# Two fused transformer layers on one core: one weight matrix loaded in four pieces, constant matmuls at three places, another order of the row loads

## The chip, the core and the metric

The kernel runs on one core of a Trainium2 chip. The engines have names of their own in the profile: PE is TensorE (matrix products, with PEld for its weight loads), DVE is VectorE, ACT is ScalarE, POOL is GpSimd, SP is SyncE, which here only issues transfers. DMA transfers are issued from the queues of SP, POOL and ACT. The metric is the device time of one execution in microseconds (us); the median of three runs is compared.

## The reference, cut to what matters

```python
def A(x, mem0, Wq, Wk, Wv, Wo):            # x [2048,512], mem [8,512], 32 heads of 128
    mem = mem0
    for s in range(64):                     # segments of 32 tokens
        h = concat([mem, x[32*s : 32*s+32]])                    # 40 rows
        q, k, v = h @ Wq, h @ Wk, h @ Wv                        # per head
        p = softmax(where(mask, q @ k.T * 128**-0.5, -1e9))     # token rows causal, memory rows over all
        o = (p @ v) @ Wo
        mem = o[:8];  out[s] = o[8:]
def B(x, wqkv, wo):                         # 32 heads of 16, no causal mask
    q, k, v = split(x @ wqkv)
    phi = lambda t: where(t > 0, t + 1, exp(t)) + 1e-6
    kv, z = sum_s phi(k) v^T, sum_s phi(k)
    return (phi(q) @ kv / (phi(q) . z + 1e-6)) @ wo
x = x + A(layernorm(x));  x = x + B(layernorm(x))               # layer 0
x = x + A(layernorm(x));  x = x + B(layernorm(x))               # layer 1, same weights
```

The mask is `(row < 8) | (row >= column)`. The eight memory rows go from segment to segment, so the 64 segments of A are a serial chain in each layer. B needs all rows of x before it can give any.

## The kernel before, in words

**Work and names.** Each layer has 64 steps, one per segment. A step projects rows of its segment to keys and queries (`kq0`, `kq1`: two halves of 16 heads), projects values (`v`), does the attention of the memory rows (`mem0`, `mem1`, the function `mem_attention`), gives the output rows by Wo (`out`) and writes the new memory rows (`next`, the function `next_mem`). This is the chain. Beside it run the attention of the token rows (`x`, the function `x_attention`), which nothing in the chain waits for, the residual (`res`), and the "left" blocks (`left0`, `left1`, `leftv`): keys, queries and values of the last 8 tokens of four segments, 32 rows made at once for a tile of 128 rows; a step's own projections take the 8 memory rows and the other 24. B is spread over the steps: after every fourth step a finished tile of 128 rows goes through `b_in` (layernorm, keys, values and queries by wqkv, running sums kva and za). After the last tile `b_mid` folds kva into wo and forms zf from za; `b_out` then gives the rows tile by tile. In layer 0 these outputs are spread over the steps of layer 1; in layer 1 all sixteen tiles come at the end (lines 2785 to 2821). For some tiles ("late") the queries are not done in `b_in`: the normalized rows are stored (`xn_scratch`) and read back transposed.

**Tiles.** A projection of 32 rows runs as groups of four matmuls, each on 32 columns of the array and 512 wide (lines 2154 and 2042; 2042 is the same with weights already in the array). Results are in one of eight PSUM banks and are copied by ScalarE (line 1919) or VectorE (line 1920). VectorE transposes 32x32 blocks (line 2173). Weights of A, 4 MB each, stay in SBUF; Wo comes in sixteen pieces of 256 KB, wqkv in one load of 1.5 MB.

**What sets the order.** The table `PLACE` (lines 16 to 1547) has for every operation a number, and a letter `a` or `v` where ScalarE or VectorE was chosen for a copy. The operations are emitted on each engine in the order of these numbers (`schedule`, line 1673); the numbers are no waits, and an engine runs its instructions in order. The bank of a tile is the least recently used one in that order. Semaphore waits follow from reads and writes. The numbers `lat` and `lands` in the code were used when the table was made, and have no effect on the program that is emitted.

**Opening.** SP issues Wk, Wq, Wv, the pieces of Wo and wqkv in this order (`load`, line 1951). ScalarE issues mem0, then x tile 0 (lines 1946, 1947); GpSimd issues x tile 1 after four constants and x tile 2 three constants later (line 1936). Then come the layernorms of these tiles, their transposes on TensorE (line 2109), and the key and query projections of the left blocks of tiles 0 to 2 (`first_left_blocks`: `sk` and `sq`) mixed with those of segment 0.

**End.** `last_rows` issues on SP, once Wq and Wk are no longer needed, transposed loads into their places: the stored queries of tiles 0 to 3 (`pq`, line 2754), the stored rows of the late tiles 4 to 7 (`xn`, line 2746), `pq` of tiles 8 to 11 and of 12 to 14, then the rows of x in four loads (`xs`, line 2753). `last_queries` makes the queries of tiles 4 to 7. The same queue carries the `dx` loads, which move rows of the output `y_sb` to the place where the residual (line 2485) adds them. The last tile's `b_in` needs the last memory step, `b_mid` needs the last tile, and the products of line 2718 and the rows of `b_out` follow.

## Time and profile before

| what | value |
|---|---|
| median of 3 runs | 1581.24 us (1580.29 to 1581.54) |
| the profiled execution's own time | 1580.13 us |
| its span | 1578.4 us |
| mean granted clock of TensorE | 0.997 |
| TensorE busy | 1511.5 us, 96% |
| VectorE busy | 1223.1 us, 77% |
| ScalarE busy | 987.4 us, 63% |
| landing of Wk, Wq, Wv after issue | 13.7, 24.4, 34.1 us |
| wqkv, issue to landing | 10.0 us |
| first key projection | 16.27 us |
| first product of line 2718 in the end | 1552.30 us |

The span is the time between the first and the last instruction in the profile; 1.7 us of the execution lie outside it. Busy time is the sum over instructions of an engine. The granted clock is 1.00 when TensorE runs at full speed. Rows of windows give, for a stretch of time, the busy time of each engine with its number of instructions in brackets, the granted clock, the DMA share and the rate.

### The profile page before, as it was taken

Reading aid. Unit: us, or ns where it says so; the run is one execution under the profiler, and the core shown is the slowest. Engines: PE = TensorE matmul, PEld = TensorE weight load, DVE = VectorE, ACT = ScalarE, POOL = GpSimd, SP = SyncE. Lnnn points to the kernel's source line nnn. Section 1 sums busy time; section 2 is a strip of 40 time slices with the busy share of each in tenths; the row PEclk is TensorE's granted clock in tenths of the full one; section 3 lists DMA queues with packets and bytes.
Section 4 is the critical chain, followed back from the end, with each engine's and each line's share of the span. In section 5 each row is a group of like instructions: output and inputs, shape, how many; then the busy total and the mean of one; then the engine's idle time right before and its main releaser. Section 6 shows DMA issues by size and latency. Waiting matters only on the chain.

```text
span 1578.4 us, 97381 instructions
## 1 busy us (share of the span) xinstructions
PE 1511.5 (96%) x48481; PEld 822.8 (52%) x40705; DVE 1223.1 (77%) x3536; ACT 987.4 (63%) x3043; POOL 197.2 (12%) x396
## 2 busy tenths in 40 slices
PE   5899999999999999999999999999999999999997
PEld 2445555555555555555545555555555455555554
DVE  4577878887777788777878787888877787777778
ACT  2566665656666666665666666666576666576665
POOL 2011110111111011111111110111101011110110
PEclk9999999999999999999999999999999999999999
DMA  9301010110000000101310111111101111001124
GB/s 381 104 20 20 17 33 20 27 24 23 21 18 16 22 24 24 24 17 30 62 32 17 26 25 20 25 29 21 31 10 27 27 27 23 23 20 20 34 42 134
DMA packets 84819, 60.69 MB, mean 38 GB/s; under 512 B 64121, under 2 KB 78777, under 8 KB 82873
## 3 DMA queue, kind: packets, MB, share of 16 engines
q1 hardware_dynamic: 71096, 37.58, 9.7%
q0 software_dynamic: 13152, 16.75, 3.9%
q8 instruction: 349, 5.72, 1.5%
q14 instruction: 62, 0.50, 0.1%
q10 hardware_dynamic: 160, 0.14, 0.0%
HBM read 25.57 MB, written 11.67 MB: 24 GB/s over the span
## 4 chain that ended last, share of the span: by engine, by line
PE 83%; DVE 8%; ACT 4%; DMA 3%; issue 1%; POOL 0%; SPq 0%; DVEq 0%
PE pb L2154 31%; PE pb L2042 21%; PE pb L2408 18%; PE pb L2054 8%; PE pb L2582 2%; ACT arena_sb L1919 2%; DMA Wq_sb<-in_A_Wq_dram 2%; PE pb L2270 1%; DMA dx_sb<-y_sb 1%; DVE arena_sb L1920 1%; PE pb L2347 1%; PE pb L2436 1%; DVE arena_sb L2173 1%; DVE y_sb L2419 1%; DVE st_sb L2092 1%
## 5 line engine op out<-in xcount | busy, mean ns | idle before, releaser
L1919 ACT ACTIVATE arena_sb<-pb 128x512 bf16<-128x512 f32 (+5 forms) x1180 | 530.8, 483 | 320.4 <-PE pb L2042 162.1
L1920 DVE CAST arena_sb<-pb 128x512 bf16<-128x512 f32 (+4 forms) x591 | 297.7, 512 | 93.7 <-PE pb L2042 51.1
L2154 PE MATMUL pb<-Wk_sb,arena_sb 128*32 128x512 bf16 x4192 | 364.4, 383 | 5.5 <-ACT arena_sb L1919 3.3
L2408 PE MATMUL pb<-Wo_sb,arena_sb 128*32 128x256 bf16 x10368 | 337.6, 273 | 4.4 <-DVE arena_sb L2318 2.1
L2173 DVE STREAM_TRANSPOSE arena_sb<-arena_sb 128x256 f32<-128x256 f32 x640 | 266.2, 432 | 48.7 <-ACT arena_sb L1919 41.2
L2054 PE MATMUL pb<-arena_sb 128*32 128x128 bf16 (+2 forms) x10800 | 277.0, 208 | 14.8 <-DVE arena_sb L1920 4.9
L2408 PEld LDWEIGHTS pb<-Wo_sb,arena_sb 128*32 128x32 bf16 x10368 | 258.1, 96 | 48.7 <-DVE arena_sb L2318 14.7
L1936 POOL DMA_DIRECT2D dx_sb<-y_sb x246 | 125.3, 513 | 1152.4 <-DVE y_sb L2419 627.0
L2054 PEld LDWEIGHTS pb<-arena_sb 128*32 128x32 bf16 x10800 | 190.1, 95 | 147.5 <-issue 33.3
L2154 PE MATMUL pb<-Wq_sb,arena_sb 128*32 128x512 bf16 x3088 | 259.5, 382 | 1.5 <-DMA Wq_sb<-in_A_Wq_dram 0.4
L2042 PE MATMUL pb<-Wv_sb,arena_sb 128*32 128x512 bf16 x2560 | 251.6, 378 | 0.1
L2154 PE MATMUL pb<-Wv_sb,arena_sb 128*32 128x512 bf16 x2560 | 251.5, 378 | 0.1
L2154 PEld LDWEIGHTS pb<-Wk_sb,arena_sb 128*32 128x32 bf16 x4192 | 112.9, 97 | 193.2 <-issue 102.6
L2042 PE MATMUL pb<-Wq_sb,arena_sb 128*32 128x512 bf16 x2032 | 199.3, 380 | 0.0
L2154 PEld LDWEIGHTS pb<-Wq_sb,arena_sb 128*32 128x32 bf16 x3088 | 83.8, 97 | 97.2 <-issue 44.4
L1919 ACT ACTIVATE outW_sb<-pb 64x256 f32<-64x256 f32 x142 | 53.6, 378 | 106.0 <-PE pb L2408 90.1
L2419 DVE TENSOR_TENSOR y_sb<-pb,outW_sb 64x256 bf16<-64x256 f32 x162 | 68.7, 424 | 50.1 <-ACT outW_sb L1919 45.4
L2358 DVE TENSOR_TENSOR arena_sb<-arena_sb,bo_sb 128x512 bf16<-128x512 bf16 x256 | 103.5, 416 | 2.4
L2318 DVE TENSOR_TENSOR arena_sb<-pb,arena_sb 128x128 bf16<-128x128 f32 x252 | 72.9, 290 | 36.3 <-ACT arena_sb L2306 12.2
L2154 PEld LDWEIGHTS pb<-Wv_sb,arena_sb 128*32 128x32 bf16 x2560 | 70.5, 95 | 53.6 <-issue 29.5
L2042 PE MATMUL pb<-Wk_sb,arena_sb 128*32 128x512 bf16 x928 | 92.5, 379 | 0.0
L2293 DVE TENSOR_TENSOR arena_sb<-arena_sb 128x256 bf16<-128x256 bf16 x252 | 70.2, 281 | 24.2 <-ACT arena_sb L2285 21.1
(122 smaller groups left out, 1804.9 us busy)
## 6 DMA issues: line engine op xcount, KB each, us to landing
Wk_sb<-in_A_Wk_dram SPq DMA_DIRECT2D x1, 4096.0 KB, 13.7
Wq_sb<-in_A_Wq_dram SPq DMA_DIRECT2D x1, 4096.0 KB, 24.4
Wv_sb<-in_A_Wv_dram SPq DMA_DIRECT2D x1, 4096.0 KB, 34.1
Wo_sb<-in_A_Wo_dram SPq DMA_DIRECT2D x16, 256.0 KB, 7.4
xs_scratch<-x_sb POOLq DMA_DIRECT2D x32, 128.0 KB, 2.7
pq_scratch<-arena_sb POOLq DMA_DIRECT2D x27, 128.0 KB, 2.5
x_sb<-xs_scratch POOLq DMA_DIRECT2D x16, 128.0 KB, 3.3
dx_sb<-y_sb SPq DMA_DIRECT2D x126, 12.0 KB
```

The lines of the kernel that those rows point to most:

```text
L1919: return e.activation(o() if callable(o) else o, i() if callable(i) else i, ACTF.Copy)
L1920: return e.tensor_copy(o() if callable(o) else o, i() if callable(i) else i)
L1936: add(eng, lambda e: e.dma_start(o, i), 0.55 if eng == "pool" else 0.66, reads=reads, writes=writes, dsem="%s%d" % (kind, k), lat=lat + (0 ...
L2042: return pe.add_instruction(mybir.InstMatmult(name=nc.get_next_instruction_name(), engine=mybir.EngineType.PE, ins=[pe.lower_ap(x), pe.low ...
L2054: r = pe.matmul(o[q], w[:, q], x, start=start, stop=stop, skip_group_check=True, tile_position=(0, 32 * j))
L2154: r = pe.matmul(o, blk[:, c, :], w, start=(c == 0), stop=(c == 3), tile_position=(0, 32 * j))
L2173: add("dve", lambda v: v.transpose(dst, src(img[:, k, :].bitcast(F32))), 0.445, reads=[("img", k, h) for h in range(2)], writes=[dkey])
L2293: add("dve", lambda v: v.tensor_tensor(Pm[:, k, :].rearrange("p (a j x) -> p a j x", a=2, j=4), PQ[:, r2, b, 0:64].rearrange("p (a x) -> p ...
L2318: add("dve", lambda v: v.tensor_tensor(oTb[:, s % NO, 16 * b:16 * b + 16, 0:8].rearrange("p (i j) q -> p j i q", i=4), heads(pv.f32()[:, 0 ...
L2358: add("dve", lambda v, b=b: v.tensor_tensor(Pbx[:, :, b, :].rearrange("p j (k x) -> p j k x", k=4), px[:, b, :].rearrange("p (k x) -> p k ...
L2408: r = pe.matmul(tl.f32()[32 * j:32 * j + 32, 0:256], oT[:, 4 * hh + n, :], Wo_sb[:, 8 * n + hh, 256 * d:256 * d + 256], start=(hh == 0 and ...
L2419: add("dve", lambda e: e.tensor_tensor(y, tl.f32()[a, 0:256], outW[c, v, :], ALU.add), c_dve(256), reads=[("outW", w), "y0"], tiles=[tl], ...
```

## The change

1. wqkv is no longer loaded by one transfer behind Wo. Four transfers of 384 KB are issued on SP, none before `next_mem` of segment 0, 1, 2 or 3 of layer 0, and each waits for the one before. On SP the first stands behind the transposed load of step 6's `prepare`, the second and third behind the `dx` load of step 2, the fourth behind those of step 4 and ahead of the transposed load of the first `b_in`.
2. `spin` is rewritten and called. One unit is twelve matmuls of 128x512 on a constant tile of ones, whose result nobody reads. Eight units stand ahead of the first key projections and wait for x tile 0; four stand between the keys and the queries of the opening; two ahead of the products of `b_mid` in layer 1; two (`spin2`) ahead of the first row output of layer 1.
3. In `last_rows` the load of the late rows (`xn`) is issued first, ahead of all `pq`.
4. `PLACE` has new numbers in steps 0 to 22 of layer 0 and from step 41 of layer 1 on; between them the order on each engine is the same as before. Some copies move between ScalarE and VectorE there. In the opening, ScalarE issues x tile 0 ahead of mem0, and GpSimd issues x tiles 2 and 1 ahead of all constants.

TensorE has 6639 scheduled operations instead of 6623, VectorE 3529 instead of 3536, ScalarE 3052 instead of 3045, SP 370 instead of 373, GpSimd 392 as before. The diff without the table; of the table the entries of three places are shown, ahead of it.

```diff
+    (0, -3, 'spin'): '12342 12989 14375 15100 15105 15679 16327 16974',
+    (0, 0, 'ldqkv'): '66837',
-    (0, 0, 'sk'): '19390 21116 22196 23282 23707v 24430',
+    (0, 0, 'sk'): '17622 17837 18269 18919 19230v 21508',
-    (0, 0, 'sq'): '29183 29399 30910 31773 32197a 32838',
+    (0, 0, 'sq'): '27549 29276 29923 30571 32514a 32731',
...
@@ -1959,7 +1967,7 @@
         for n in range(4):
             hs = slice(8 * n + 2 * i, 8 * n + 2 * i + 2)
             load(Wo_sb[:, hs, :], A_Wo[hs].rearrange("h e d -> e h d"), ("Wo", i, n), 36.45 + 3.0 * i + 0.75 * n, "dWo%d" % i)
-    load(wqkv_sb[:, :, :], B_wqkv.rearrange("(c p) f -> p c f", p=128), "wqkv", 51.5)
+    P.count += 1
 
     def load_wo_b(n):
         add("pool", lambda e: e.dma_start(MB_sb[:, :, :], B_wo.rearrange("(c p) f -> p c f", p=128)), 1.1, after=[late[-1]],
...
@@ -2054,27 +2062,27 @@
                 r = pe.matmul(o[q], w[:, q], x, start=start, stop=stop, skip_group_check=True, tile_position=(0, 32 * j))
         return r
 
-    SPIN = {}
     LATE = {0: (8, 9, 10, 11, 12, 13, 6, 7, 4, 5), 1: (4, 5, 6, 7)}
-    def spin(layer, step, name, units, cols=512, fresh=0):
+    def spin(layer, step, name, n, after=(), reads=(), fresh=1):
 
         P.at(layer, step, name)
-        tl = P.tile()
-
-        def mm(pe):
-            x = one_sb[:, 0:128].unsqueeze(1).to_broadcast([128, cols // 128, 128])
-            for i in range(units):
-                for j in range(4):
-                    o, q = tl.f32()[32 * j:32 * j + 32, 0:cols], slice(32 * j, 32 * j + 32)
-                    if 4 * i + j < 4 + fresh:
-                        r = pe.matmul(o, one_sb[:, q], x, start=True, stop=True, skip_group_check=True, tile_position=(0, 32 * j))
-                    else:
-                        r = again(pe, o, one_sb[:, q], x, True, True, (0, 32 * j), True)
-            return r
-        before = [o for o in P.nodes[-40:] if o.engs == ("pe",)]
-        nd = add("pe", mm, units * (cols / 2.4 + 3.0) * 1e-3, reads=["one"], tiles=[tl])
-        nd.order.update(before)
-        return nd
+        for i in range(n):
+            tl = P.tile()
+
+            def mm(pe, tl=tl):
+                x = one_sb[:, 0:128].unsqueeze(1).to_broadcast([128, 4, 128])
+                for u in range(3):
+                    for j in range(4):
+                        o, q = tl.f32()[32 * j:32 * j + 32, 0:512], slice(32 * j, 32 * j + 32)
+                        if u < fresh:
+                            r = pe.matmul(o, one_sb[:, q], x, start=True, stop=True, skip_group_check=True, tile_position=(0, 32 * j))
+                        else:
+                            r = again(pe, o, one_sb[:, q], x, True, True, (0, 32 * j), True)
+                return r
+            nd = add("pe", mm, c_pe(3, 512), reads=["one"] + list(reads), tiles=[tl])
+            nd.order.update(after)
+            after = [nd]
+        return after
 
     ln_no = [0]
 
...
@@ -2210,11 +2218,21 @@
 
         def first_left_blocks():
 
+            done = []
+            last = spin(0, -3, "spin", 8, reads=[("x", 0)], fresh=3)
             for W, key, move, nm in ((Wk_sb, "Wk", left_keys, "sk"), (Wq_sb, "Wq", left_queries, "sq")):
                 for G in range(3):
                     for b in range(2):
                         at(2 * G + b, nm)
+                        n0 = len(P.nodes)
                         move(G, b, project(hTL[lroom(G)], [("hTl", lroom(G))], (W, key, b, True))[0])
+                        pe = [n for n in P.nodes[n0:] if n.engs == ("pe",)]
+                        if G == 0:
+                            for n in pe:
+                                n.order.update(last)
+                            done += pe
+                if nm == "sk":
+                    last = spin(0, -1, "spin", 4, done)
             for G in range(2):
                 at(4 * G - 2, "leftv")
                 left_values(G)
...
@@ -2548,6 +2566,11 @@
             w_of[s] = out_block(s)
             if s + 1 < NSEG:
                 next_mem(s)
+            if first and s < 4:
+                nd = P.nodes[-1]
+                at(s, "ldqkv")
+                add("sp", lambda e, s=s: e.dma_start(wqkv_sb[:, s, :], B_wqkv.rearrange("(c p) f -> p c f", p=128)[:, s, :]), 0.45,
+                    after=[nd], writes=["wqkv"], dsem="dqkv%d" % s, lat=4.0)
             if s > 0:
                 residual((s - 1) // 4, (s - 1) % 4, w_of[s])
                 if g == 0:
...
@@ -2694,6 +2717,9 @@
 
     def b_mid(layer, step):
 
+        hold = []
+        if layer == 1:
+            hold = spin(layer, step, "spin", 2, [n for n in P.nodes[-40:] if n.engs == ("pe",) and n.key[2] == "bi"])
         P.at(layer, step, "bm")
         km, kk = half(qTl[:, 0], 1), ("qTl", 0, 1)
         add("dve", lambda v: v.tensor_tensor(km.rearrange("p (c m x) -> p c m x", c=4, m=4),
...
@@ -2716,7 +2742,7 @@
         for c in range(4):
             tl = P.tile()
             add("pe", lambda pe, c=c, tl=tl: tiled(pe, tl.f32()[:, :], km[:, 128 * c:128 * c + 128], MB_sb[:, c, :], True, True),
-                c_pe(1, 512), reads=[kk, ("MB", c)], tiles=[tl])
+                c_pe(1, 512), reads=[kk, ("MB", c)], tiles=[tl]).order.update(hold)
             evac(MB_sb[:, c, :], lambda tl=tl: tl.f32()[:, :], 512, tiles=[tl], writes=[("MB", c)])
 
 
...
@@ -2738,14 +2764,14 @@
         rows = [n for n in P.nodes if n.key[:3] == (1, step - 1, "lr") and n.engs == ("dve",)]
 
         prev = None
-        for w, (vw, nm, free, t0) in enumerate(((pq_view, "pq", [], 3.4), (xs_view, "xs", rows, 3.4))):
-            for i in range(0, NT - 1, 4):
+        for w, (vw, nm, free, t0) in enumerate(((pq_view, "pq", [], 7.5), (xs_view, "xs", rows, 5.0))):
+            for i in sorted(range(0, NT - 1, 4), key=lambda i: w or i not in LATE[1]):
                 n = min(4, NT - 1 - i)
                 P.at(1, step + i // 4, "ld" + nm)
                 if not w and i in LATE[1]:
                     nd = add("sp", lambda e, i=i: e.dma_start_transpose(XN(i), xn_view[i:i + 4].rearrange("t p d -> (t p) d")), 2.6,
                              reads=[("xn", t) for t in range(i, i + 4)], writes=[("RE", i), ("RE", i + 1)], after=P.res["Wk"][1],
-                             dsem="dlxn%d" % i, lat=4.8)
+                             dsem="dlxn%d" % i, lat=8.0)
                     if prev is not None:
                         nd.order.add(prev)
                     prev = nd
...
@@ -2754,7 +2780,7 @@
                          if w else (lambda e, vw=vw, i=i, n=n: e.dma_start_transpose(
                              XQ[:, :, i:i + n, :].rearrange("p c t x -> p c (t x)"), vw[i:i + n].rearrange("t p d -> (t p) d"))), 0.6 if w else 2.6,
                     reads=[(nm, t) for t in range(i, i + n)], writes=[("XE", w, t) for t in range(i, i + n)],
-                    after=P.res["Wq"][1] + free, dsem="dl%s%d" % (nm, i), lat=t0 + 0.22 * i)
+                    after=P.res["Wq"][1] + free, dsem="dl%s%d" % (nm, i), lat=t0)
                 if prev is not None:
                     nd.order.add(prev)
                 prev = nd
...
@@ -2788,7 +2814,12 @@
                 y = tiled(pe, td.f32()[:, o], zf_sb[:, c, :], e[:, c, :], True, True)
             return y
         qk = [("XQ", t // 4 * 4, fc) for fc in range(4)] if last and t in LATE[1] else []
-        add("pe", md, c_pe(4, 128), reads=["zf"] + ek + qk, tiles=[td])
+        nd = add("pe", md, c_pe(4, 128), reads=["zf"] + ek + qk, tiles=[td])
+        hold = []
+        if last and t == 0:
+            c, place = P.count, P.place
+            hold = spin(layer, step, "spin2", 2, [nd])
+            P.place, P.count = place, c
         if not last and t == 0:
             was = [n for key in rk for n in [P.res[key][0]] + P.res[key][1] if n is not None] if all(key in P.res for key in rk) else []
             for h in range(2):
...
@@ -2814,7 +2845,7 @@
         add("dve", lambda v: v.tensor_tensor(e, e, quarters(rb), ALU.mult), c_dve(512), reads=ek + rk + qk, writes=ek)
         for c in range(4):
             add("pe", lambda pe, c=c: tiled(pe, ty.f32()[:, :], e[:, c, :], MB_sb[:, c, :], c == 0, c == 3),
-                c_pe(1, 512), reads=ek + [("MB", i) for i in range(4)], tiles=[ty])
+                c_pe(1, 512), reads=ek + [("MB", i) for i in range(4)], tiles=[ty]).order.update(hold)
         add("dve", lambda v: v.tensor_tensor(x, x, ty.f32()[:, :], ALU.add), c_dve(512), reads=[xk], writes=[xk],
             tiles=[ty])
         if last:
```

3060 rows, old and new, of the table PLACE are left out of this document.

## Prediction

> **What bounds the kernel now.** I read the page first, then the windows and the chain of waits of the first 60 us, then the same for the last 50 us, and last the seam between the re-ordered and the untouched part. The page:
>
> ```profile
> span 1578.4 us, 97381 instructions
> PE 1511.5 (96%) x48481; PEld 822.8 (52%) x40705; DVE 1223.1 (77%) x3536; ACT 987.4 (63%) x3043; POOL 197.2 (12%) x396
> ...
> q8 instruction: 349, 5.72, 1.5%
> ...
> PE 83%; DVE 8%; ACT 4%; DMA 3%; issue 1%; POOL 0%; SPq 0%; DVEq 0%
> ```
>
> TensorE is the bound: 1511.5 of 1578.4 us busy, 83% of the chain that ended last. Removing work of other engines buys nothing in the middle; what can be won is TensorE's 67 us of idle time and its slow clock, and most of both lies at the two ends. Instructions come in packets of 5.72 MB / 349 = 16 KB. The windows of the opening (TensorE, weight loads, VectorE, ScalarE, GpSimd, then granted clock, DMA share, GB/s):
>
> ```profile
> 24.00:26.00 2.00, 0.85 (x13) 0.24 (x17) 0.93 (x6) 1.33 (x3) 0.00 (x0) 1.00 0.98 410
> 26.00:28.00 2.00, 2.00 (x28) 0.84 (x24) 1.17 (x3) 1.23 (x3) 0.00 (x0) 0.55 1.02 426
> 28.00:30.00 2.00, 2.00 (x28) 0.81 (x24) 0.48 (x1) 0.00 (x0) 0.00 (x0) 0.60 1.00 418
> ...
> 48.00:50.00 2.00, 2.00 (x73) 1.50 (x61) 0.86 (x4) 0.94 (x2) 0.00 (x0) 1.00 0.84 316
> 50.00:52.00 2.00, 0.00 (x0) 0.00 (x0) 0.20 (x1) 0.00 (x0) 0.00 (x0) 1.00 0.10 37
> 52.00:54.00 2.00, 1.61 (x34) 0.51 (x26) 0.39 (x2) 0.98 (x2) 0.00 (x0) 0.87 0.04 8
> 54.00:56.00 2.00, 2.00 (x24) 0.67 (x16) 0.47 (x1) 0.47 (x1) 0.00 (x0) 0.50 0.00 0
> 56.00:58.00 2.00, 2.00 (x36) 0.88 (x28) 1.06 (x4) 0.78 (x3) 0.00 (x0) 0.77 0.00 0
> ```
>
> Twice TensorE stands still and then runs at half clock for about 3.4 us (26.3 to 29.7 and 53.6 to 57.0). Half clock for 3.4 us loses 1.7 us. The second time it is preceded by 2 us in which nothing runs at all. The timeline of TensorE says what each stop waited for:
>
> ```profile
> 25.77 0.40 PE L2154 MATMUL pb<-Wq_sb,arena_sb 128*32 128x512 bf16 x4 [0.36 <-DMA Wq_sb<-in_A_Wq_dram]
> ...
> 52.01 0.24 PE L2054 MATMUL pb<-arena_sb 128*32 128x128 bf16 x3 [2.01 <-issue]
> ```
>
> "issue" means that no semaphore was waited for. One instruction packet, begun at 49.74, took 1.16 us there, at the end of a load phase of 316 to 426 GB/s; wqkv is the last load in it (issued 41.5, landed 51.5). In the tail:
>
> ```profile
> 1552.00:1554.00 2.00, 1.83 (x40) 0.93 (x36) 1.88 (x4) 1.32 (x2) 0.00 (x0) 0.50 0.33 110
> 1554.00:1556.00 2.00, 1.71 (x60) 1.27 (x52) 1.58 (x4) 1.58 (x3) 0.00 (x0) 0.66 0.04 8
> ...
> 1565.00:1570.00 5.00, 5.00 (x144) 2.83 (x140) 5.00 (x9) 4.97 (x10) 0.00 (x0) 1.00 0.26 81
> ```
>
> The clock halves once more for 3.4 us, but VectorE, busy 5.00 of 5.00 from 1560 on, sets the end there.
>
> **The change, part by part.** Sums are against the profiled execution: span 1578.4 and 1.7 us around it, 1580.13. The median of the three runs, 1581.24, is 1.1 above; I add the same difference at the end.
>
> *wqkv in four pieces.* Its 1.57 MB leave the opening: at 350 GB/s (the rate of the windows from 36 to 44 us) 4.5 us, so the load phase ends near 45.5, not 50. The packet at 49.74 then meets no traffic, and the stall goes: -2.0 (bounds 0 and -2.0). TensorE then does not pause before 53.6, and the half clock goes with it: -1.7 (bounds 0 and -1.7). The last piece stands on SP behind the dx rows of step 4, whose issues ended at 98.7, and before the transposed load of 104.5. At 1.1 us for its bytes and 2.5 to 3.3 for the smaller loads of the page's list it lands by 104; the first matmul with wqkv (line 2582) ran at 109.4. So 5 us cover it: 0, up to +1.2 if SP's transposed load moves by one issue (0.7) and the use with it.
>
> *Filler in the opening.* Eight fillers of three groups of four 128x512 matmuls stand behind the first transposes, ahead of the key projections; four more are between keys and queries. A group takes 0.43 us at half clock and 0.22 at full (rows at 54.21 and 53.06 of the chain). 8 groups cold and 16 warm are 7.0 us. x0 becomes ScalarE's first load, x2 GpSimd's: issued 0.6 and 2.3 us earlier. VectorE's first operation (10.26, waiting for rows of x) moves up by 0.6 to 2.3, the first transposes from 13.24 to 10.9 to 12.6. I take 12.6, as x0's row is the nearest. Keys then begin at 19.6, not 16.27, all at full clock. 30 groups, 12 groups of filler and two transposes follow before the first query group: 6.6 + 2.6 + 0.9, to 29.7; the remaining 23 groups take 5.0, to 34.7. Before, key and query projections ended at 33.5: +1.2, or -0.5 with the earlier transposes. Behind it lies slack, TensorE's idle 1.6 us at 35.6 to 37.2 and Wv, which lands at 36.0 in both. I take +0.3; the ends are -1.0 and +2.3 (no slack used and the four later fillers half cold).
>
> [...]
>
> *The seam.* Layer 0 up to step 22 and layer 1 from step 41 are re-ordered; between them each engine's order is identical. At step 22 the new order puts on VectorE, between the query and key transposes of segment 22, the copies of the left value block, query, key and two output blocks, and one layernorm's statistics. From the rows of before (copy of 512 columns 0.68, half 0.38, transpose 0.45, statistics 0.65 + 0.18, scaling 0.38) that stretch is 6.7 us instead of 4.2, with ScalarE idle beside it. TensorE executes in order and has little queued that does not depend on it: +1.9 (bounds 0, if TensorE finds work, as the 15.83 busy of 16 us there before suggests it had, and +2.5). The identical order behind it carries the delay on.
>
> *Untouched stretch.* Only the numbers of PSUM banks differ; the least recently used one is taken in the same order: 0 (bounds ±0.8, about half of the 1.75 us that TensorE idles in the 98 us from 302 to 400).
>
> *Layer 1 from step 41.* One wait of VectorE for a dx row at 1365.6 idles 1.4 us and may move: -0.3 (bounds -1.4 and +0.5).
>
> *Tail.* The rows of the late queries go first on SP. SP's rows of before:
>
> ```profile
> 1530.82 1.86 SPq L2754 DMA_TRANSPOSE Wq_sb<-pq_scratch  x1
> 1532.72 3.62 SPq L2746 DMA_TRANSPOSE Wk_sb<-xn_scratch  x1
> 1536.39 0.74 SPq L1936 DMA_DIRECT2D dx_sb<-y_sb  x1
> 1537.17 7.63 SPq L2754 DMA_TRANSPOSE Wq_sb<-pq_scratch  x2
> ```
>
> The dx load of the last segment then stands behind one transpose, not two; VectorE waited 1.17 us for it (line 2485, until 1541.49). All pq transposes and xs rows come behind it: three at 3.8 and four rows, done near 1550, still ahead of their first use at 1555.9. Filler before the last products (3 groups each, 0.65 to 1.29 us) can save the half clock: twelve products took 1.47 instead of 0.65. Two fillers before the first row output cost 1.3 us where TensorE waits for VectorE. VectorE's sum grows by 0.3. Together -0.7 (bounds -2.2 and +1.3).
>
> **Sum:** -2.0 - 1.7 + 0 + 0.3 + 1.9 + 0 - 0.3 - 0.7 = -2.5: 1577.6 for a profiled execution, 1578.7 for the median. About 0.2%, 3.2 us, is what a measurement here can tell from no change, so this is "within".
>
> **Rivals.**
>
> *Seam and opening cost little.* TensorE fills step 22 with other work (+0.5) and earlier rows of x gain 1.0: -2.0 - 1.7 - 1.0 + 0.5 - 1.0 = -5.2, 1576.0. For it: 15.83 of 16 us busy at the seam; against it: the VectorE sum.
>
> *The stall stays.* It was not the traffic, or the next packet meets the four pieces. Then neither 2.0 nor 1.7 is won: -2.5 + 3.7 = +1.2, 1582.4. For it: the packet took 1.16 us but the stall 2.01, so 0.9 is unexplained. [...] Against it: of the stops in this trace called issue, the large ones (50.0 and 1540.9) both have a slow instruction packet beside heavy DMA.
>
> *Slower: filler stays cold.* Place: TensorE from 12.6 to the end of the query projections. 24 groups at 0.43 are 10.3 us instead of 7.0, the twelve later ones 5.2 instead of 2.6: queries end 3.3 + 2.6 = 5.9 later than the 34.7 above, at 40.6, past Wv and past all slack, 7.1 after the 33.5 of before. Net -2.5 - 0.3 + 7.1 = +4.3, 1585.5. It decides when keys start after about 22. For it: transposes and waits stand between the first fillers; against: before, the clock rose within 3.4 us of the first dense matmuls.
>
> **How the numbers follow.** Forecast 0.48 (its own range 1576.5 to 1580.8; faster in 0.19, within in 0.29); cheap seam 0.16, faster; stall stays 0.18 (within 0.14, slower 0.04); cold filler 0.18 (slower 0.15, within 0.03, if part of it is hidden). Faster 0.35, within 0.46, slower 0.19. The range 1574.5 to 1585.0 takes the forecast, the cheap seam and the staying stall with their bounds, and about a third of the cold filler, which is spread around its 1585.5.
>
> **What would show it.** Right: no stop named issue near 50 us, clock 1.0 from the keys on, load phase over by 46, memory chain of segment 0 about 3 us earlier; a VectorE-bound stop of about 2 us near 290; VectorE full from 1555 on. Wrong: keys after 22, half clock past 30, an issue stop elsewhere in the first 60 us, TensorE waiting for wqkv at step 6, or VectorE idle in the tail for xs rows.

## The result

The changed kernel takes 1582.91 us (median of 21 runs, 1579.93 to 1587.57), the kernel before 1578.58 us (21 runs, 1575.40 to 1584.23) beside it on the same chip: ratio 1.0025, 95% interval 1.0016 to 1.0033. By that ratio it is slower by 3.9 us (2.5 to 5.2). The forecast was a ratio of 1578.7 / 1581.24 = 0.9984. Its sign was wrong.

The page of the changed kernel, the lines that answer to those shown of before:

```profile
span 1580.0 us, 97710 instructions
PE 1518.3 (96%) x48673; PEld 825.5 (52%) x40833; DVE 1229.9 (78%) x3529; ACT 983.8 (62%) x3050; POOL 198.1 (13%) x396
...
q8 instruction: 351, 5.75, 1.6%
...
PE 82%; DVE 8%; ACT 4%; DMA 3%; issue 2%; POOL 1%; SPq 0%; DVEq 0%; POOLq 0%
```

TensorE is busy 6.8 us longer: sixteen fillers of three groups at 0.22 us are 10.6, and part of before's busy time was work at half clock that is gone. TensorE's share of the chain fell from 83% to 82% and "issue" (waits without a semaphore) rose from 1% to 2%. The windows of the opening (same columns as before):

```profile
24.00:26.00 2.00, 2.00 (x44) 0.75 (x28) 0.62 (x1) 0.00 (x0) 0.00 (x0) 1.00 1.06 438
26.00:28.00 2.00, 2.00 (x44) 0.47 (x20) 1.34 (x5) 1.68 (x3) 0.00 (x0) 1.00 0.95 393
...
46.00:48.00 2.00, 2.00 (x101) 1.87 (x94) 1.78 (x5) 0.77 (x2) 0.00 (x0) 1.00 0.16 50
48.00:50.00 2.00, 1.52 (x36) 0.50 (x20) 0.72 (x3) 0.38 (x1) 0.00 (x0) 1.00 0.03 8
50.00:52.00 2.00, 2.00 (x40) 0.68 (x28) 0.46 (x2) 0.86 (x3) 0.00 (x0) 1.00 0.00 0
```

This part went as forecast. The load phase is over by 46 (50 GB/s in the window from 46; before, 316 in that from 48), the stop near 50 is gone, and the granted clock is 1.00 in every window from 24 us to the end of the opening. The loss lies elsewhere. I cut both profiles where VectorE writes a step's results into the output rows (line 2419 before, 2437 after). For the stretch of identical order the other kernels below give the spread.

| stretch | before (two to three profiles with that order) | after | difference |
|---|---|---|---|
| start to output of segment 1 | 64.01, 62.50, 60.83 | 59.58 | -2.9 |
| to step 13 | 137.60, 137.18, 136.77 | 136.56 | -0.6 |
| steps 13 to 20 | 80.52, 80.30, 80.80 | 81.57 | +1.0 |
| steps 20 to 22 (seam) | 22.24, 22.24, 22.24 | 25.27 | +3.0 |
| step 22 to the end of layer 0 (identical order) | 464.5 to 468.6 over kernels with this order | 467.36 | chance |
| layer 1 to step 40 (identical order) | 496.8 to 503.1 | 497.20 | chance |
| layer 1, steps 40 to 62 | 258.9 in the mean of kernels with the old order | 259.71 | +0.8 |
| step 62 to the end | 51.3 in the mean of twelve kernels (50.6 to 52.0) | 52.79 | +1.5 |

The sum is +2.8 us, within the measured 2.5 to 5.2. The identical stretches move by up to 3 us either way from one profile to the next, so one profile's span says little about 0.25%: all that follows goes by medians of runs and by the local durations. Not every row of the table stands clear of that scatter. Steps 20 to 22 take 22.23 to 22.26 us in all twelve profiles with the old order there. But steps 13 to 20 take 80.55 to 81.57 in the five profiles with the new order and 80.28 to 81.23 in twelve with the old one (means 81.1 and 80.7), and steps 40 to 62 take up to 259.46 with the old order.

TensorE's waits over 1 us in the seam and in the end of the changed kernel:

```profile
290.04 0.55 PE L2605 MATMUL pb<-arena_sb 128*32 128x512 bf16 x4 [1.10 <-DMA arena_sb<-arena_sb]
298.31 0.24 PE L2062 MATMUL pb<-arena_sb,one_sb 128*32 128x128 bf16 x4 [1.43 <-DVE arena_sb L2311]
...
1542.15 0.40 PE L2426 MATMUL pb<-Wo_sb,arena_sb 128*32 128x256 bf16 x7 [1.92 <-issue]
...
1554.40 0.68 PE L2062 MATMUL pb<-Wq_sb,arena_sb 128*32 128x128 bf16 x35 [1.41 <-issue]
```

(Lines of the changed kernel: 2605 is the first product with wqkv, 2582 before; 2062, 2426 and 2437 are 2054, 2408 and 2419 before; 1928 is VectorE's copy, 1920 before.) At 290.04 TensorE waits for a transposed load, at 298.31 for VectorE; the two stops in the end wait for no semaphore.

### The profile page after: what moved, and what is told of

The parts are those of the page before. It is cut to its first block, busy times and chain, and to the rows that moved or that the text cites. A ratio compares the mean times of both kernels' runs of the same rounds, so it can differ in the third digit from the quotient of the medians.

```text
span 1580.0 us, 97710 instructions
## 1 busy us (share of the span) xinstructions
PE 1518.3 (96%) x48673; PEld 825.5 (52%) x40833; DVE 1229.9 (78%) x3529; ACT 983.8 (62%) x3050; POOL 198.1 (13%) x396
## 4 chain that ended last, share of the span: by engine, by line
PE 82%; DVE 8%; ACT 4%; DMA 3%; issue 2%; POOL 1%; SPq 0%; DVEq 0%; POOLq 0%
PE pb L2162 30%; PE pb L2050 20%; PE pb L2426 17%; PE pb L2062 8%; DMA dx_sb<-y_sb 2%; PE pb L2605 2%; ACT arena_sb L1927 1%; PE pb L2288 1%; DVE arena_sb L1928 1%; DVE y_sb L2437 1%; PE pb L2365 1%; DVE arena_sb L2181 1%; PE pb L2454 1%; DVE st_sb L2100 1%; ACT outW_sb L1927 1%
## 5 line engine op out<-in xcount | busy, mean ns | idle before, releaser
L1927 ACT ACTIVATE arena_sb<-pb 128x512 bf16<-128x512 f32 (+5 forms) x1170 | 523.0, 480 | 316.0 <-PE pb L2050 157.0
L1928 DVE CAST arena_sb<-pb 128x512 bf16<-128x512 f32 (+4 forms) x603 | 307.8, 518 | 87.1 <-PE pb L2050 49.6
L2307 ACT ACTIVATE arena_sb<-pb 128x160 bf16<-128x160 f32 x256 | 78.0, 307 | 20.0 <-PE pb L2288 9.0
```

Of the source, the lines that this page charges most:

```text
L1927: return e.activation(o() if callable(o) else o, i() if callable(i) else i, ACTF.Copy)
L1928: return e.tensor_copy(o() if callable(o) else o, i() if callable(i) else i)
L2307: add("act", lambda a: a.activation(PQ[:, r2, b, 64:224], tl.f32()[:, 64:224], ACTF.Exp, scale=SCALE), c_act(160), tiles=[tl], writes=[("P ...
```

## The experiments

All kernels take code and numbers of `PLACE` from the two kernels; the numbers are renumbered from the start, so only their order counts. A figure with a star is a single execution.

| kernel | median us | kernel before beside it | ratio, 95% |
|---|---|---|---|
| before_again | 1577.74* | 1579.87 | |
| head_only | 1581.57 | 1579.87 | 1.0018 [1.0006, 1.0030] |
| head_14 | 1575.47 | 1579.87 | 0.9973 [0.9958, 0.9987] |
| tail_only | 1581.01 | 1579.87 | 1.0005 [0.9991, 1.0019] |
| h14_nofill | 1577.26 | 1578.84 | 0.9988 [0.9973, 1.0002] |
| h14_whole | 1580.42 | 1578.84 | 1.0007 [0.9994, 1.0021] |
| pieces_only | 1578.73 | 1579.81 | 0.9997 [0.9988, 1.0006] |
| seam_act | 1577.81 | 1578.84 | 0.9995 [0.9981, 1.0009] |
| seam_xn | 1581.87* | 1579.59 | |
| seam_both | 1578.41 | 1579.59 | 1.0003 [0.9985, 1.0022] |
| h14_mid | 1577.22 | 1579.59 | 0.9989 [0.9971, 1.0007] |
| h14_end | 1577.41 | 1578.84 | 0.9997 [0.9982, 1.0013] |
| h14_end_nofill | 1580.52 | 1579.59 | 1.0003 [0.9988, 1.0018] |
| h14_end_bm | 1580.02 | 1579.81 | 1.0000 [0.9986, 1.0015] |
| head_14_more | 1578.80 | 1579.81 | 0.9994 [0.9984, 1.0005] |
| h14_phase | 1590.75 | 1579.81 | 1.0076 [1.0060, 1.0091] |
| h14_no4 | 1593.87 | 1578.68 | 1.0082 [1.0055, 1.0109] |
| h14_no8 | 1594.97 | 1578.68 | 1.0098 [1.0068, 1.0128] |

### The two halves: head_only, head_14, tail_only

head_only is the changed kernel up to step 22 of layer 0 and the order before from there on. Against the changed kernel:

```diff
         hold = []
-        if layer == 1:
-            hold = spin(layer, step, "spin", 2, [n for n in P.nodes[-40:] if n.engs == ("pe",) and n.key[2] == "bi"])
...
-            for i in sorted(range(0, NT - 1, 4), key=lambda i: w or i not in LATE[1]):
+            for i in range(0, NT - 1, 4):
...
-        if last and t == 0:
-            c, place = P.count, P.place
-            hold = spin(layer, step, "spin2", 2, [nd])
-            P.place, P.count = place, c
```

> The change's opening, four loads of wqkv, filler there and new order of steps 0 to 22, with the end of before. Theory R: opening gains about 1, the seam at step 22 costs 2.9, so 1.5 to 3.5 us slower than before. Theory U: opening gains 4 to 5.5, seam costs 2.9, so 1 to 3 us faster. Theory K (the untouched stretch loses, by other banks): 1 to 3 slower, but with a seam of 2.9 and a further loss of 3 us spread over steps 23 to 63 in its profile.

head_14 differs from it only in the order of steps 14 to 22, which is that of before (one entry of several):

```diff
-    (0, 22, 'kq0'): '24340 24360 24370 24390 24450a 24570v 24440v 24520v',
+    (0, 22, 'kq0'): '24350 24360 24370 24410 24550a 24630v 24500a 24610v',
```

> As head_only, but the order of before comes back at step 14, ahead of the seam of step 22, so that the seam's copies stand where they stood. All theories: 2.9 us faster than head_only. Against before: theory R -1 to +0.5 us, theory U -4 to -5.5, theory K about 0 with a gain of 4 to 5 up to step 14 that is lost again behind it.

tail_only has the opening of before, and the change from step 41 of layer 1 on. Against the changed kernel:

```diff
-            last = spin(0, -3, "spin", 8, reads=[("x", 0)], fresh=3)
+            last = []
...
-    P.count += 1
+    load(wqkv_sb[:, :, :], B_wqkv.rearrange("(c p) f -> p c f", p=128), "wqkv", 51.5)
...
-            if first and s < 4:
+            if False:
```

> The opening and steps 0 to 22 of before, with the change's order from step 41 of layer 1 on, its order of the row loads and its two fillers at the end. By the profiles of the pair the end lost 2.0 to 2.4 us from step 41 on. Theories R and U: 1 to 2.5 us slower than before. If the loss of the end is chance (waits for dx rows), within 1 us.

With them the kernel before was profiled once more:

> The kernel before, profiled once more. Theory R (rare stall): the stop of 2.01 us at 50 us and the half clock after it are an accident of the one profiled execution, whose 1580.13 lies 1.5 above the median of all its runs; the new profile has no stop over 0.5 us there, no half clock from 53.6 to 57.0, and the output rows of segment 0 come about 3 us earlier after 49.8. Theory U (usual stall): the same stop of 1.5 to 2.5 us and the same half clock show again, at the same instruction.

head_only was 2.8 us slower than before and tail_only 0.8 slower (-1.4 to +3.0); the sum of 3.6 is close to the whole change's 3.9. Between head_only and head_14 lie 6.1 us in the medians and 3.6 to 4.3 in the local durations (steps 13 to 22: 106.85 against 102.53 and, in the repeat below, 103.29). So the order of steps 14 to 22 costs more than the whole opening gains. The repeat of before shows the opening's stop again (2.34 us at the same instruction) but a clock of 1.00 behind it:

```profile
52.00:54.00 2.00, 1.43 (x35) 0.56 (x27) 0.39 (x2) 0.98 (x2) 0.00 (x0) 1.00 0.03 8
54.00:56.00 2.00, 2.00 (x44) 0.90 (x36) 1.21 (x3) 0.93 (x3) 0.00 (x0) 1.00 0.00 0
56.00:58.00 2.00, 2.00 (x68) 0.84 (x44) 1.79 (x6) 1.34 (x5) 0.00 (x0) 1.00 0.00 0
```

The forecast had taken the half clock at 54 to 57 for a property of the kernel; it was one of that execution. tail_only, the third profile with this opening, stops for 0.98 us and shows none there either.

### The opening: h14_nofill, h14_whole, pieces_only

All but the last start from head_14. h14_nofill takes the twelve fillers of the opening away:

```diff
-            last = spin(0, -3, "spin", 8, reads=[("x", 0)], fresh=3)
+            last = []
...
-                if nm == "sk":
-                    last = spin(0, -1, "spin", 4, done)
```

> head_14 without the twelve fillers of the opening (the three loads of x in their new order, and wqkv in four pieces, stay). Theory F (filler pays): half clock returns for about 3.4 us from the first keys and once more near 26 to 30 us; the output rows of segment 1 come 1.5 to 3 us later than head_14's 59.0. Theory P (only the pieces of wqkv pay): segment 1 at 58.5 to 59.5, since keys start about 4 us earlier and the time is lost only before Wq lands.

h14_whole loads wqkv in one transfer behind Wo again:

```diff
-    P.count += 1
+    load(wqkv_sb[:, :, :], B_wqkv.rearrange("(c p) f -> p c f", p=128), "wqkv", 51.5)
...
-            if first and s < 4:
+            if False:
```

> head_14 with wqkv in one load behind Wo again. Theory P: TensorE stops near 49 to 50 us for 1 to 2.3 us with nothing waited for, while the load phase lasts to 50, and segment 1's output rows come at 60.0 to 61.5 instead of 59.0. Theory F: no stop over 0.5 us, 59.0 to 59.5.

pieces_only is the kernel before with the four pieces alone:

```diff
-    load(wqkv_sb[:, :, :], B_wqkv.rearrange("(c p) f -> p c f", p=128), "wqkv", 51.5)
+    P.count += 1
...
+            if first and s < 4:
+                nd = P.nodes[-1]
+                at(s, "ldqkv")
+                add("sp", lambda e, s=s: e.dma_start(wqkv_sb[:, s, :], B_wqkv.rearrange("(c p) f -> p c f", p=128)[:, s, :]), 0.45,
+                    after=[nd], writes=["wqkv"], dsem="dqkv%d" % s, lat=4.0)
```

> The kernel before with wqkv in four pieces as in the change, and nothing else: the order of the steps, the fillers and the order of the loads of x stay as before. If the pieces are what takes the stop of the opening away, no stop named issue is near 50 us, the first two memory rows come 2.0 to 2.4 us earlier (the row of segment 1 near 60.3 instead of 62.5), the first `b_in` waits for no weights, and the time falls by 1.5 to 2.4 us. Rival: the stop moves to another block and the time is the same.

The stop hangs on the load. With one transfer it comes back, though the fillers and the order of the opening are those of the change; timeline of TensorE and a window of h14_whole:

```profile
50.75 0.39 PE L2156 MATMUL pb<-Wv_sb,arena_sb 128*32 128x512 bf16 x1 [1.24 <-issue]
```

```profile
48.00:50.00 2.00, 1.50 (x43) 0.80 (x31) 0.88 (x3) 0.68 (x2) 0.00 (x0) 1.00 0.77 286
50.00:52.00 2.00, 0.88 (x21) 0.43 (x17) 0.49 (x2) 0.00 (x0) 0.00 (x0) 1.00 0.18 64
```

The output of segment 1 comes at 61.38 there, at 59.00 and 59.98 in two profiles of head_14: the pieces are worth 1.4 to 2.4 us. With the pieces alone (pieces_only) it comes at 60.68, 1.8 earlier than the 62.45 of three profiles with the opening of before, and no stop over 0.6 us is near 50. Its median is 1.1 us lower, its interval (-1.9 to +0.9 us) reaches across zero. The fillers are worth 0.3 us (59.79 without them against 59.49): not told from zero. They were to cover the half clock at 26 us, which the profile of before shows (0.55 in the window from 26). The repeat of before has the same stop of 1.64 us ahead of 26 us and no drop there; it drops at 37.3 us instead, behind a stop of 1.62:

```profile
26.00:28.00 2.00, 2.00 (x40) 1.02 (x44) 0.91 (x3) 1.39 (x4) 0.00 (x0) 1.00 1.01 422
...
38.00:40.00 2.00, 2.00 (x31) 0.49 (x12) 0.88 (x3) 0.80 (x3) 0.00 (x0) 0.50 1.10 348
```

The place changes, but each has a drop. All five profiles without the twelve fillers run 3.4 us at half clock from some point between 24.9 and 37.3 us (before, its repeat, tail_only, pieces_only, h14_nofill), each within 2 us of a stop of 1.6 to 2.1 us. Of the thirteen profiles with all twelve fillers two do (h14_end_nofill at 36.5, seam_xn at 37.9), though all have a stop of 2.08 us that ends between 35.8 and 37.7. So the fillers do what they were put there for, but the output of segment 1 hardly shows it.

What sets a drop off behind one such stop and not behind another is not shown; no run here isolates it.

### The seam: seam_act, seam_xn, seam_both

These start from head_only. seam_act puts five copies of steps 20 to 22 back on ScalarE:

```diff
-    (0, 22, 'kq0'): '24340 24360 24370 24390 24450a 24570v 24440v 24520v',
+    (0, 22, 'kq0'): '24340 24360 24370 24390 24450a 24570v 24440a 24520v',
-    (0, 22, 'kq1'): '24460 24510 24590 24700 24480 24490 24540 24580 24730v 24770v 24720v 24660a 24840v',
+    (0, 22, 'kq1'): '24460 24510 24590 24700 24480 24490 24540 24580 24730a 24770v 24720v 24660a 24840v',
...
```

> head_only with five copies of steps 20 to 22 (a value block, the query and one key block of segment 22, two output blocks of step 21) on ScalarE again, as before, all else in the same order. Theory V (VectorE's load makes the seam): the two steps 20 to 22 take 25.8 us in head_only and 22.2 in before; here 22.5 to 24, and the kernel is 2 to 3.5 us faster than head_only. Theory O (TensorE's new order makes the seam): 25 to 26 as in head_only, no gain.

seam_xn moves the store of the normalized rows of tile 4 on GpSimd (last number of the entry) behind the `dx` load of step 21, where before has it too; seam_both does both:

```diff
-    (0, 22, 'bi'): '23610v 23620v 23650a 23660a 23690v 24020 23810 24230 24310 24880 24940 25280a 25330v 25370v 25550v 26390 25620 26570v 25780v 0 0 0 23880',
+    (0, 22, 'bi'): '23610v 23620v 23650a 23660a 23690v 24010 23810 24220 24300 24880 24940 25280a 25330v 25370v 25550v 26390 25620 26570v 25780v 0 0 0 24530',
```

> head_only with one issue moved: the 128 KB store of the normalized rows of tile 4 stands on GpSimd's queue behind the dx issue of step 21, as before, not beside the transposed load of the same rows. Theory Q (the store slows that load, and TensorE, which has the load's first user queued ahead of the next memory rows, waits): the transposed load lands in 4.2 to 4.5 us, not 5.6 to 6.2; TensorE's wait for it (1.1 to 1.7 us) is gone; steps 20 to 22 take 24.0 to 24.5 us, not 25.3 to 25.8. Theory N (chance): no change, 25.2 to 25.9.

> seam_xn and seam_act together. If the seam is the sum of the store and of VectorE's five copies: steps 20 to 22 take 23.0 to 23.6 us (22.2 before, 25.8 in head_only), and the kernel is 1.5 to 4 us faster than before. If copies and store hide each other, 24 or more.

Steps 20 to 22 take 22.24 us before, 25.27 in the changed kernel, 25.81 in head_only, 24.73 in seam_act, 25.27 in seam_xn and 23.91 in seam_both. The forecast had named only VectorE's copies. What it missed is a collision of transfers: the new order issues the 128 KB store of tile 4 0.3 us after the transposed load that tile 4's first product with wqkv waits for, where before issues it 5.7 us after. The DMA issues between 282 and 292 us of the changed kernel (KB each, us from issue to landing), then the same list of before, from 286 to 296 us:

```profile
xn_scratch<-arena_sb POOLq DMA_DIRECT2D x1, 128.0 KB, 2.8
x_sb<-in_A_x_dram POOLq DMA_DIRECT2D x1, 128.0 KB, 5.0
pq_scratch<-arena_sb POOLq DMA_DIRECT2D x1, 128.0 KB, 4.6
arena_sb<-arena_sb SPq DMA_TRANSPOSE x1, 5.6
```

```profile
pq_scratch<-arena_sb POOLq DMA_DIRECT2D x1, 128.0 KB, 3.4
xn_scratch<-arena_sb POOLq DMA_DIRECT2D x1, 128.0 KB, 2.6
arena_sb<-arena_sb SPq DMA_TRANSPOSE x1, 4.3
```

The transposed load lands 5.6 us after its issue instead of 4.3 (6.2 in head_only), and TensorE waits 1.10 us at line 2605 (1.66 in head_only), with the memory rows of segment 22 queued behind it. With the store moved (seam_xn) the load lands after 2.4 us. That is less than the 4.3 of before with the same two transfers behind it, which stays open. But at the same place another stop takes most of the gain:

```profile
292.04 0.38 PE L2603 MATMUL pb<-arena_sb 128*32 128x512 bf16 x1 [1.05 <-issue]
```

The copies are the other half of what could be found: with them on ScalarE the wait for VectorE behind the memory rows falls from 1.43 to 0.63. Timeline of TensorE in seam_act:

```profile
290.30 0.56 PE L2603 MATMUL pb<-arena_sb 128*32 128x512 bf16 x4 [1.35 <-DMA arena_sb<-arena_sb]
297.77 0.24 PE L2060 MATMUL pb<-arena_sb,one_sb 128*32 128x128 bf16 x4 [0.63 <-DVE arena_sb L2309]
```

The wait for the load (1.35) stays, as it should. So of the 3.6 us of head_only's seam the copies are about 1.1 and the pair about 1.9. Of the 1.7 that stay in seam_both, two stops are 1.13:

```profile
288.08 0.38 PE L2603 MATMUL pb<-arena_sb 128*32 128x512 bf16 x1 [0.50 <-issue]
295.37 0.24 PE L2060 MATMUL pb<-arena_sb,one_sb 128*32 128x128 bf16 x4 [0.63 <-DVE arena_sb L2309]
```

Two such stops plus about 0.5 us give the seam of every kernel with the new order: 1.10 + 1.43 in the changed kernel (+3.0), 1.66 + 1.44 in head_only (+3.6). The 0.5 is TensorE's own work in the new order, busy 22.2 us in these steps instead of 21.6; it was not tried alone.

### The last steps: h14_mid, h14_end, h14_end_nofill, h14_end_bm

From head_14. h14_mid has the change's order in steps 41 to about 60 of layer 1 (one entry of many):

```diff
-    (1, 51, 'kq0'): '123660 123670 123680 123690 123750a 123930v 123810v 123820v',
+    (1, 51, 'kq0'): '123660 123670 123730 123770 123860a 123940v 123890v 123920v',
```

> head_14 with the change's order of steps 41 to about 60 of layer 1, and the end of before. Theory D (the new order lets VectorE reach the residual adds earlier, so that it waits longer for dx rows): steps 40 to 62 take 259.3 to 259.9 us instead of 257.9 to 258.8, the loss at steps 45 and 50 to 51, and the kernel is 0.5 to 1.5 slower than head_14. If these losses were chance: 258.0 to 258.8.

h14_end has the change's order from about step 61 on, with the late rows first and the four fillers (the reverse of the first diff above):

> head_14 with the change's end: its order from step 61 of layer 1 on, the late rows first on SP, and the fillers. If the end costs, as the pair of profiles has it, from the output rows of step 62 to the last instruction 52.0 to 52.8 us, where the kernels with the end of before have 50.8 to 52.0; 0.3 to 1.5 us slower than head_14. My prediction's step said the end gains 0.7: then 50.0 to 51.3.

h14_end_nofill is the same without the fillers:

```diff
-        if layer == 1:
-            hold = spin(layer, step, "spin", 2, [n for n in P.nodes[-40:] if n.engs == ("pe",) and n.key[2] == "bi"])
...
-        if last and t == 0:
-            c, place = P.count, P.place
-            hold = spin(layer, step, "spin2", 2, [nd])
-            P.place, P.count = place, c
```

> h14_end without the four fillers of the end. From the output rows of step 62 to the last instruction h14_end took 53.5 us. Theory I (one block of TensorE's instructions arrives late in the middle of the last memory rows, because of the order and where the blocks of 256 instructions end, not because of fillers): a stop called issue of 1.5 to 2.2 us stays at line 2426's place or close to it, and 52.5 to 53.5. Theory F2 (the fillers cost): 51.5 to 52.3.

h14_end_bm moves three products of `b_mid` ahead of the products of the rows' denominators:

```diff
-    (1, 66, 'bm'): '138110v 137940 137990v 138000v 138010v 138030v 138040v 138160 138270v 138170 138340v 138150 138200v 138250 138310v',
+    (1, 66, 'bm'): '138050v 137940 137990v 138000v 138010v 138030v 138040v 138070 138270v 138080 138340v 138060 138200v 138250 138310v',
```

> The kernel with the change's opening, the old order from step 14 on and the change's order of the last steps without fillers (1580.52 us, from the memory row of step 62 to the end 53.5 us against 51.2 as the mean of the kernels with the old end), with one more edit: on TensorE the three products of b_mid that fold the first block into wo (numbers 11, 7 and 9 of `bm`) stand ahead of the first three row groups of the products of line 2062 (numbers 0 of `bl` for the last tile and two others), not behind them. If the order of these products is what costs time at the end, the first copy of the folded wo comes about 28.3 us after the memory row of step 62 instead of 30.0, and the end 51.8 to 52.3 us after it, the whole 1579.0. If the stops of TensorE at a block of 256 instructions are the cause, they stay (at the same count of instructions), and the end stays at 53.0 to 54.0 us.

From the output of step 62 to the end: 51.94 and 51.96 in head_14, 51.99 in tail_only, 52.79 in the changed kernel, 53.53 in h14_end, 53.54 without its fillers, 53.90 with the products moved. Leaving out the fillers changes nothing in this pair, in which the granted clock drops to 0.50 16 to 17 us after the output of step 62 with and without them. My theory that the order of the products costs the time fell too: the first copies of the folded wo came 0.9 us earlier, the end did not. The middle (h14_mid) stays at 259.11, 0.2 from the old order's mean: nothing.

What the rows do show is a trade. The late rows first do what the forecast said on SP: the `dx` load stands behind one transpose of 2.89 us, not two. SP's queue in the changed kernel:

```profile
1532.30 2.89 SPq L2772 DMA_TRANSPOSE Wk_sb<-xn_scratch  x1
1535.23 0.74 SPq L1944 DMA_DIRECT2D dx_sb<-y_sb  x1
1536.02 8.99 SPq L2780 DMA_TRANSPOSE Wq_sb<-pq_scratch  x3
```

VectorE's wait for that row, 1.17 us before, is gone. But that wait was not the last one in the kernel before. VectorE's rows there:

```profile
1541.49 0.42 DVE L2485 TENSOR_TENSOR x_sb<-x_sb,dx_sb 96x512 bf16<-96x512 bf16 x1 [1.17 <-DMA dx_sb<-y_sb]
...
1543.17 0.70 DVE L2092 BATCH_NORM_STATS2 st_sb<-pb 128x6 f32<-128x512 f32 x1 [0.49 <-PE pb L2054]
```

Behind the `dx` row it waits another 0.49 us for TensorE, which stopped for 1.09 us (issue) ahead of 1541.99, and the layernorm of the last tile (line 2092) begins 16.41 us after the output of step 62. In the changed kernel TensorE's stop of 1.92 us lies inside the last output projection (line 2426, shown above), VectorE waits 2.47 us for its result, and that layernorm begins after 16.69 us:

```profile
1543.00 0.43 DVE L2437 TENSOR_TENSOR y_sb<-pb,outW_sb 64x256 bf16<-64x256 f32 x1 [2.47 <-ACT outW_sb L1927]
...
1555.34 0.69 DVE L1928 CAST arena_sb<-pb 128x512 bf16<-128x512 f32 x1 [1.40 <-PE pb L2062]
```

`b_mid` then starts 25.2 us after the output of step 62; in the twelve profiles with the end of before it is 24.8 to 25.1. So up to there nothing was won, and little lost. Behind it the second stop (1.41 us at 1554.40) leaves VectorE idle for 1.40 in a stretch where it waits 0.42 at most in head_14's repeat. From the start of `b_mid` to the end the changed kernel takes 27.6 us and tail_only, with a second stop of 0.92 us, 27.1. The twelve profiles with the old end take 25.8 to 26.3 there when the granted clock stays at 1.00 (five of them), and 26.0 to 26.9 when it drops to 0.50 for 3.4 us (seven, before among them). That the second stop makes the end slower is argued from these rows; no run took it away alone. One profile shows an end without such stops: h14_no8 of the next section, with the old order and no stop over 0.7 us called issue behind step 62, has the layernorm after 15.63 us and the shortest end of all twenty, 49.77.

### Blocks of 256 instructions: h14_phase, h14_no4, h14_no8, head_14_more

Counting all of TensorE's instructions in the trace from the start (matmuls, weight loads and some 330 that only wait for semaphores), every stop of 0.9 us or more called issue, 38 in all twenty profiles of this study, stands ahead of an instruction whose number is 192 more than a multiple of 256 (within 4): 1216 (50 us) and 88000 (1540.9) before, 88256 and 88768 in the changed kernel, and the 1.05 us of seam_xn. A block is here the 256 instructions from one such number to the next, and an edge the place where it begins. The queue of instruction packets moves 5.72 MB in 349 packets, 16 KB each. h14_phase shifts the count: head_14 with eight fillers that load their weights once, not three times, which is 64 instructions less near 15 us and nothing else:

```diff
-            last = spin(0, -3, "spin", 8, reads=[("x", 0)], fresh=3)
+            last = spin(0, -3, "spin", 8, reads=[("x", 0)], fresh=1)
```

> The kernel with the change's opening and the old order from step 14 on (1575.47 us), with eight fillers of the opening that load their weights once instead of three times: 64 fewer weight loads on TensorE near 15 us, and everything behind them at a count lower by 64. It stops for 1.65 us near 1537.6 us ahead of instruction 88256 of TensorE, which is 192 more than a multiple of 256. Theory (a block of 256 instructions arrives late beside transposed loads): the stop stays at a count that is 192 more than a multiple of 256, so it falls on an instruction that is 64 further on in the program's work, or on another block. Rival (the place in the work decides, as a transfer or a wait that the profile does not show): the stop stays ahead of the same matmul, at count 88192. The time stays within 2 us of 1575.5 in both.

head_14 was timed again beside it:

> The kernel with the change's opening and the old order from step 14 on again, in more rounds: it was 4.4 us faster than the kernel before (0.9973), while its opening as the sum of the local durations gives 2.8 to 3.2 us. If the opening is all that it gains, the ratio lies between 0.9975 and 0.9990; if the earlier number is the size, 0.9965 to 0.9980.

The stop kept its number, 88256, and so moved to another instruction, as the theory had it. Unexpected was the time: 12 us more than head_14 beside it, spread over the kernel. More than half of it, 7.1 us, lies between step 22 and the end of layer 0, where the order is identical (475.65 us; 464.5 to 468.6 in all kernels with the old count). Two more kernels shift the count by other means. h14_no4 leaves out the four later fillers (64 instructions less), h14_no8 the eight first (192 less, which is 64 more by multiples of 256):

```diff
-                if nm == "sk":
-                    last = spin(0, -1, "spin", 4, done)
```

> The kernel with the change's opening and the old order from step 14 on, without the four fillers between the keys and the queries of the opening: 64 TensorE instructions less ahead of everything that follows, as in the run with weights loaded once (1590.75 us, 12 us slower than with 64 more), but by other instructions. Theory (the position of the blocks of 256 instructions in the work sets what TensorE loses at their edges): the interval ahead of the first instruction of a block is again about 0.10 us in the mean, not 0.05, and the time 1588 to 1593. Rival (the fillers' own content, or chance, made that run slow): 1576 to 1580, and 0.05 us.

```diff
-            last = spin(0, -3, "spin", 8, reads=[("x", 0)], fresh=3)
+            last = []
```

> The same kernel without the eight fillers ahead of the keys and with the four behind them: 192 TensorE instructions less, which for blocks of 256 is the same as 64 more. Theory: the edges fall on other instructions than in both other kernels, the mean interval at them differs from 0.05 us by more than 0.01 in one direction or the other (the direction is not known beforehand), and the time follows it by that difference times 330 blocks, between 0.5 and 0.8 of which reaches the end. Rival: 0.05 us and 1576 to 1580, as with all twelve fillers and with none.

Both are slower still, by 14 and 16 us against head_14 (from the ratios 1.0082, 1.0098 and 0.9994). The group of the output projections, out of the list of costliest groups on TensorE (busy time, mean ns, idle before and what ended it), of head_14's repeat, of h14_phase and of h14_no8:

```profile
L2424 PE MATMUL pb<-Wo_sb,arena_sb 128*32 128x256 bf16 x10368 | 336.7, 273 | 4.4 <-issue 2.2 <-DVE arena_sb L2334 0.7
```

```profile
L2424 PE MATMUL pb<-Wo_sb,arena_sb 128*32 128x256 bf16 x10368 | 342.4, 273 | 12.6 <-issue 10.1 <-DVE arena_sb L2334 1.2
```

```profile
L2423 PE MATMUL pb<-Wo_sb,arena_sb 128*32 128x256 bf16 x10368 | 344.0, 273 | 11.9 <-issue 9.1 <-DVE arena_sb L2333 0.9
```

The same matmuls are preceded by 10.1 and 9.1 us of issue stops instead of 2.2. Over the first 328 blocks that begin behind 83 us, the interval ahead of the first instruction of a block sums to 17.1 us in head_14's repeat and to 34.5, 35.1 and 37.7 us in the three shifted kernels, with 33 to 36 stops over 0.4 us instead of 10. At eight other places in the block the same sum is 4.8 to 7.3 us in head_14's repeat. Before has 15.4 us at the edges and the changed kernel 15.3. h14_nofill, with 256 instructions less, has 15.4 and is not slower than before (0.9988). So the position of the block edges is the cause, by three kernels and three ways to shift it; the 17 to 21 us more at the edges reach the end to about three quarters. Of the stops over 0.4 us, 19 to 21 in each shifted kernel stand ahead of matmuls or weight loads of the output projections, and 5 in head_14's repeat. Why an edge costs more in one place than in another is open.

The median interval at an edge is 2 ns, in the kernel before and in the changed one, but the sum over the edges decided up to 16 us.

head_14 itself gave 0.9973 and, in the repeat, 0.9994; the two intervals barely overlap. Their middle, 0.17% or 2.6 us below before, fits the 2.9 to 3.5 us of the opening's local durations. Its first timing is the only one here whose interval lies below 1; that of the repeat reaches 1.0005.

## Why the prediction was wrong

**Stall of the opening, -2.0: right.** Gone with the load, back with it (h14_whole 1.24 us). The rival "the stall stays" is out.

**Half clock behind it, -1.7: failed.** The term counted one execution's accident. Of three profiles with that opening one shows it, and its drop behind the stop is its second in the opening; the other two have one each, at 37.3 and 24.9 us. The forecast read a row of one profile as the kernel's; 1.7 us is of the size by which executions differ.

**Four pieces, 0: right.** The first product with wqkv waits for no weights. (SP issues three transfers more than before, 373 instead of 370.)

**Filler of the opening, +0.3: mechanism right, sign open.** The first ten groups of filler took 0.43 us each, to 15.1 us (one of them 0.77, with transposes in it), and the others 0.22. Keys began at 18.08, not 19.6, at 0.22 us a group, so the rival "filler stays cold" did not happen. Without the fillers segment 1 comes 0.3 us later; the median of h14_nofill is 1.8 us higher than that of head_14 and 1.5 lower than that of its repeat. Opening in all: -3.4 forecast; -3.5 in the rows of the changed kernel (-2.9 to segment 1, -0.6 to step 13), -3.0 in the mean of the eleven profiles with the whole new opening (59.63 and 136.98 against 62.45 and 137.18): a right total of partly wrong terms. The output of segment 1 comes at 62.45 before, 60.68 with the pieces alone, 59.79 with the earlier rows of x and the new order as well, 59.63 with the fillers. The two in the middle are single profiles and the eleven lie between 59.0 and 61.0, so the last two steps are not told from the scatter.

**Seam, +1.9: the step that failed most.** It measured +3.0 in steps 20 to 22; the +1.0 ahead of them is within the scatter. The mechanism named, VectorE's copies, is there with about 1.1 (a wait of 1.43 us of TensorE for VectorE, 0.63 with five copies back on ScalarE). The forecast looked at engines only; it did not follow the moved 128 KB store on GpSimd's queue into the time of the transposed load that TensorE needs next, which is the other wait, 1.10 us.

**Untouched stretch, 0: right, by luck.** Not because the order there is identical, but because the opening's fillers add exactly 256 TensorE instructions (8 x 24 + 4 x 16). With 64 less the same order costs 12 us more. The bounds of ±0.8 came from the idle time of TensorE, and nothing in them knew of this.

**Layer 1 from step 41, -0.3:** the rows give +0.8 in the changed kernel and +0.2 in h14_mid; within chance (up to 259.46 with the old order, 259.71 here).

**Tail, -0.7: wrong sign, +1.5.** The `dx` wait went, as forecast; what was late next was not asked. Already before, VectorE waited 0.49 us more behind it for TensorE, whose stop at a block edge ended last. In the changed kernel such a stop lies in the last output projection, the last tile's layernorm begins 0.28 us later than before, not earlier, and a second one (1.41 us) falls behind the start of `b_mid`. The half clock that the filler was to save is real: with the end of before it costs up to about 1 us behind the start of `b_mid` (26.0 to 26.9 against 25.8 to 26.3). The changed kernel and tail_only run there at full clock and still take 27.6 and 27.1. Whether their fillers kept the clock up is not shown, as five of the twelve profiles with the old end, which have none there, keep it too.

In sum, by the rows of the changed kernel: the seam was off by 1.1 (2.1 with the stretch ahead of it), the tail by 2.2 and layer 1 by 1.1 us. That is 4.4 to 5.4 of the 6.4 us between -2.5 and the measured +3.9, and the rest lies within the interval of 2.5 to 5.2. Of these the seam stands clear of the scatter, and so does the tail (52.8 to 53.9 us in four profiles with the new end, 50.6 to 52.0 with the old one), but for tail_only's 51.99.

## What to carry to other kernels

A moved transfer must be followed into the stretch where it now runs: look for the load that a bound engine waits for next, and compare their issue times (with a 128 KB store beside it, the load of the seam landed after 6.2 us in head_only; with the store moved away, after 2.4 in seam_xn). A single profile's stops and clock drops belong to that execution until a second one shows them (the drop at 53.5 us of before is in one of three profiles with that opening). Before crediting a change of order, fillers or loads with a few us, look at how many instructions it adds ahead of the bound engine's long stretch: 64 or 192 fewer cost this kernel 12 to 16 us, while 256 more or fewer cost nothing.
